# A routing tail in another order, and the first batch's tiles turned by VectorE instead of TensorE

## The chip, the core and the metric

The kernel runs on one core of a Trainium2 chip. The metric is the device time of one execution in microseconds (us), the median of several runs. The engines named below are TensorE (PE; its weight loads are PEld), VectorE (DVE), ScalarE (ACT), GpSimd (POOL) and SyncE (SP), which issues most transfers.

## What is computed

Three stages follow each other: attention with a cluster mask over 2 batches of 8 heads (768 tokens, 64 wide), a dense feed-forward stage on the 1536 tokens (512 to 2048 to 512), and a mixture of 8 experts to which each token goes by the largest of 8 gate sums. The rows of one expert are gathered in disp in token order, and a token's result is its gate weight times its row of y. The change touches the place between the second and the third stage.

```python
def reference(**kwargs):
    ...
    attn_out = _attn_ref(**attn_kwargs)
    B, H, S, D = attn_out.shape
    x = np.ascontiguousarray(attn_out.transpose(0, 2, 1, 3)).reshape(B * S, H * D)
    x = _moe_ref(x=x, **moe_kwargs)
    return _moe2_ref(x=x, **moe2_kwargs)

def _moe2_ref(x, w_gate, w1, w2, capacity):
    logits = x @ w_gate
    expert_idx = np.argmax(logits, axis=1)
    ...
    gate_w = probs[np.arange(N), expert_idx]
    ...
    h = np.maximum(np.einsum('ecd,edf->ecf', disp, w1), 0.0)
    y = np.einsum('ecf,efd->ecd', h, w2)
    ...
```

## The kernel before

**The dense stage** (class Moe) goes through 64 half-steps T, 32 for each batch of 768 tokens. Half-step T works on unit n = T // 2 (a slice of 128 of the 2048 hidden columns) and on one half of the batch's tokens. `run` issues, in this order: `finish(T)` (ScalarE's and VectorE's later work on the results of the two half-steps before), `up(T)` (12 matmuls of 384 columns into a PSUM bank called ph, L868; two such banks, m0 and m1, take turns, so `up(T)` writes the bank of `up(T-2)`), `e0(T)` (exp on ScalarE, L881; two VectorE steps, L884 and L885) and `down` (9 matmuls of 512 columns into three of six banks o, L934, for the unit two before). `finish(T)` on VectorE is L897 (the last reader of ph of T-1), L902, L911, L912, L917, and ScalarE does L895, L896 and L905 beside it. The engines run ahead of each other only as far as these banks and tiles allow.

**Steps in between.** Three times in each `finish`, behind L902 (with L905), behind L912 and behind L917, `aside` calls `Router.step`, which lets a list of jobs go on by one step: the Python generators `rest`, `prep`, `route` and `place`, one after the other. This is how the routing of the first batch is strewn between the dense stage's steps on VectorE and TensorE. The variable `K.room` is the bank of the last `up`; its columns from 384 on are free for a job.

**Routing of the first batch.** When the last unit of the first batch is added up (n = 15, at T = 34 and 35), ScalarE brings each of the six 128-token tiles out of its bank into x2 (`done`, L1156). In the half-step after, `turn` transposes the three tiles that are ready on TensorE (4 transposes each, L1177, into the same bank o), ScalarE copies each to a tile xt (L1181), and `dots` multiplies it with the gate weights wg, padded to 120 columns (4 matmuls each that run as 8, L1186). VectorE takes the 8 sums of each token (`logits`, L1195), and `route` with `place` (L1235 to L1314) finds each token's expert and place. Then GpSimd scatters the rows to DRAM (L1325).

**Routing of the second batch** is the tail: after half-step 63 the list `TAIL` gives the order by hand. F finishes a half-step, E and D are the last two units' `down` of one tile, T turns a tile, L makes its dots, V makes a tile's two parts xr (`parts`: L1169 on ScalarE, L1170 on VectorE), G and c are `route` of tiles 0 to 2 or 3 to 5 and its steps (with the matmuls called cum, L1220, behind the one-hot oh, L1247), O adds a tile's rows to expert 0 by matmuls (xet, L1482), I turns expert 0's rows of the first batch (L1468), W cuts weights (L824), s lets the jobs go on. Then the experts' stage begins with the matmuls he (L1548).

Of the kernel before, what the change touches and what calls it, by code (L numbers as in the profile page):

```python
# [10 lines left out]
F32 = mybir.dt.float32  # L11
F32R = mybir.dt.float32r
# [108 lines left out]
class Centroids:  # L121
# [17 lines left out]
    def zero(self):  # L139
        self.nc.gpsimd.memset(f32(self.K.cc), 0.0)  # L140
# [534 lines left out]
class Narrow:  # L675
# [74 lines left out]
    def run(self, c, store=True):  # L750
        for g in (self.bias, self.last, self.up, self.sign):
            g(c)
# [93 lines left out]
class Moe:  # L846
# [112 lines left out]
        self.up(T)  # L959
        self.e0(T)  # L960

    def run(self, R, out, narrow):

        self.R = R
        R.jobs.insert(0, narrow)
        self.banks()
        N = self.NB * self.NF
        L = 2 * self.LAG
        ready, late = [], None
        for T in range(L, 2 * N):  # L970
            self.finish(T, 2 * N)
            if late:
                R.logits(*late)
                if late[2] == 6:
                    R.jobs.append(R.route(late[0], 0, 6, R.l))
                late = None
            self.up(T)
            self.e0(T)
            n, half = divmod(T - L, 2)
            b, f = divmod(n, self.NF)  # L980
            if n % 2 == 1 and half == 0 and n % 16 < 8:
                R.zero(n % 16 // 2 + 4 * (n // 16), out)
            toks = range(3 * half, 3 * half + 3)
            acc = self.acc
            for o, t in ready:
                R.turn(o, t, acc[t])
            self.down(n, toks)
            for o, t in ready:
                R.dots(o, t, acc[t - t % 3], t % 3)
            if ready:  # L990
                late = (o, t - 2, t + 1, acc[t - 2])
            ready = [(b, t) for t in toks] if f == self.NF - 1 else []

    GROUPS = ((0, 3), (3, 6))
    TAIL = (
        "F0 E0 E1 E2 F1 X0 D0 D1 D2 E3 T0 E4 T1 W1 E5 V0 D3 L0 T2 V1 D4 L1 V2 V3 I0 D5 L2 G0 c04 T3 T4 L3 c01 T5 c03 "
        "L4 O0 s06 s03 V4 L5 V5 s03 G1 c14 O1 s04 c11 O2 c13 s05 O3 O4 O5"
    )

    def tail(self, X):  # L1000
# [43 lines left out]
class Router:  # L1044
# [36 lines left out]
    def prep(self):  # L1081

        nc, E = self.nc, self.E
# [5 lines left out]
            )  # L1089

        nc.gpsimd.memset(self.wg[:, :, E:WIDE], 0.0)
        for k in range(4):
            nc.sync.dma_start(
                out=self.wg[32 * k:32 * k + 32, :, 0:E],
                in_=self.w_gate[128 * k:128 * k + 128].rearrange("(j c) e -> c j e", c=32),
            )
# [7 lines left out]
        for b in range(2):  # L1104
# [13 lines left out]
            out=self.tri[:, 0, :], in_=self.tri[:, 0, :], compare_op=ALU.is_gt, fill=0.0, base=0,  # L1118
# [19 lines left out]
            out=self.seat, in0=self.seat, scalar=self.lim, in1=self.seat, op0=ALU.is_le, op1=ALU.mult  # L1138
        )

    def zero(self, i, out):

        nc = self.nc
        if i == 0:
            nc.gpsimd.memset(self.z, 0.0)
            nc.gpsimd.memset(self.z[:, 512:513].bitcast(I32), 1 << 20)
        dst, n = (self.slots, ROW) if i < 4 else (out, 512)
        r = dst.shape[0] // 4
        i %= 4
        nc.sync.dma_start(  # L1150
            out=dst[i * r:i * r + r].rearrange("(r p) c -> p r c", p=128),
            in_=self.z[:, 0:n].unsqueeze(1).to_broadcast([128, r // 128, n]),
        )
# [4 lines left out]
    def parts(self, b, t, pool):  # L1158

        x = mixed(self.x2[b][:, t, 0:512])  # L1160
        if t == 5:
            hi, lo = [pool.tile([128, 512], F32R, tag="gl", name="xr", bufs=4) for _ in range(2)]
        elif t == 3:
            hi, lo = [self.room.tile([128, 512], F32R, tag="n32", name="xr", bufs=2) for _ in range(2)]
        else:
            r = self.room.tile([128, 2, 512], F32R, tag="n64", name="xr", bufs=3)
            hi, lo = r[:, 0], r[:, 1]
        self.rows[t] = hi, lo
        self.nc.scalar.activation(out=plain(hi), in_=x, func=AF.Copy)  # L1169
        self.nc.vector.tensor_sub(out=plain(lo), in0=x, in1=plain(f32(hi)))  # L1170
# [19 lines left out]

    def view(self, lg, n):
        return lg[:, 0:WIDE * n].rearrange("p (t e) -> p t e", e=WIDE)[:, :, 0:self.E]

    def logits(self, b, t0, t1, lg):
        self.nc.vector.tensor_copy(out=self.l[:, t0:t1, :], in_=self.view(lg, t1 - t0))  # L1195

    def step(self):
        if self.jobs:
# [219 lines left out]
class Experts:  # L1418
# [40 lines left out]
    def sums(self):  # L1459
        if self.ps:  # L1460
            return False
        self.ps = [self.K.bank(f"b{2 * g + 1}", "xet", (128, 2, MAIN)) for g in range(2)]
        return True
# [236 lines left out]
def tile_program(ctx, tc, q, k, v, centroids, moe_w_in, moe_w_out, w_gate, w1, w2, capacity, out):  # L1700
    nc = tc.nc
    B, H, S, D = q.shape
    E = w1.shape[0]
    with tc.manual_schedule():
# [29 lines left out]
        with ExitStack() as c2:  # L1734
            sh.ps = sh.open_psum(tc, c2, "psm")
            R = Router(sh, nc, tc, c2, w_gate, capacity, slots, S)
            N.p = R.room = c2.enter_context(tc.tile_pool(name="late", bufs=2))
            for c in range(N.CUT, min(N.CUT + 3, N.N)):
                N.load(c)
            M.run(R, out, N.rest())  # L1740
            X = Experts(sh, nc, tc, xp, p, W, u0, R, out, E)
            M.tail(X)
            X.run()
            Overflow(sh, nc, tc, p, X, R, w1, w2).run(R.z)
# [32 lines left out]
```

## Time and profile before

| what | value |
|---|---|
| median of 3 runs | 775.38 us (774.37 to 775.41) |
| the profiled execution | 775.32 us, its span 773.2 us |
| TensorE | 749.7 us busy, 97% of the span |
| VectorE | 598.0 us, 77% |
| ScalarE | 466.6 us, 60% |
| GpSimd | 226.5 us, 29% |
| granted TensorE clock | 0.995 of full speed on the mean |

The profiled execution is 2.1 us longer than its span, the time before the first and behind the last instruction. A busy TensorE is one that has a matmul in its pipeline, and ends of matmuls are modelled: the distance from one matmul's start to the next tells more than the length of one. Idle time of an engine is put down to the one that ended the wait.

### The profile page before, as it was taken

How to read it: one execution, taken by the hardware profiler on the slowest of the kernel's cores; microseconds unless marked ns; L12 is line 12 of the kernel's file. 1: busy time of each engine (PE TensorE's matmuls, PEld its weight loads, DVE VectorE, ACT ScalarE, POOL GpSimd, SP SyncE). 2: the span in 40 equal slices, each digit the busy share in tenths (PEclk: the TensorE clock that was granted, in tenths of full speed). 3: DMA queues.
4: the chain of work that ended last, by engine and by line, in shares of the span. 5: the costliest groups of instructions: out<-in, count | busy, mean ns of one | idle time of the engine just before them, and what ended most of it. 6: DMA issues, size and time to landing. Idle time of an engine off the chain costs nothing.

```text
span 773.2 us, 12411 instructions
## 1 busy us (share of the span) xinstructions
PE 749.7 (97%) x4219; PEld 601.9 (78%) x4219; DVE 598.0 (77%) x1190; ACT 466.6 (60%) x901; POOL 226.5 (29%) x254
## 2 busy tenths in 40 slices
PE   8999999999999999999999999999999999999994
PEld 5665566666655668889999999999888999899993
DVE  5756779788777799999996788888677676677761
ACT  4445778778677776666656454545646655656651
POOL 6276677787689200010000021000031101101111
PEclk9999999999999999999999999999999999999997
DMA  8797698999885529688474455341429968998640
GB/s 186 157 220 150 164 276 233 231 235 250 233 245 168 218 65 379 254 290 305 179 271 151 150 191 191 117 153 58 137 99 265 270 213 232 288 252 226 208 127 22
DMA packets 125753, 155.77 MB, mean 201 GB/s; under 512 B 35538, under 2 KB 91442, under 8 KB 121588
## 3 DMA queue, kind: packets, MB, share of 16 engines
q1 hardware_dynamic: 120960, 131.82, 60.6%
q0 software_dynamic: 4688, 23.09, 7.4%
q8 instruction: 35, 0.57, 0.3%
q14 instruction: 34, 0.28, 0.1%
q10 hardware_dynamic: 36, 0.01, 0.0%
HBM read 93.65 MB, written 42.24 MB: 176 GB/s over the span
## 4 chain that ended last, share of the span: by engine, by line
PE 76%; DVE 13%; issue 5%; ACT 3%; DMA 1%; POOL 0%; ACTq 0%; POOLq 0%; DVEq 0%; SPq 0%
PE ph L868 13%; PE o L934 12%; PE he L1548 10%; PE y L1580 10%; PE acc L437 8%; PE pm L374 5%; PE pst L404 4%; PE pst L407 3%; PE psim L260 3%; DVE m L378 2%; PE psum L450 1%; DVE n L885 1%; DVE cut L824 1%; PE pt L242 1%; PE o L1186 1%
## 5 line engine op out<-in xcount | busy, mean ns | idle before, releaser
L824 DVE TENSOR_TENSOR cut<-raw,cut 128x512 fp32r<-128x512 f32 x168 | 110.0, 685 | 23.4 <-ACT cut L821 9.5
L378 DVE TENSOR_REDUCE m<-pm 128x1 f32<-128x768 f32 x96 | 91.3, 955 | 47.0 <-PE pm L374 46.4
L425 POOL TENSOR_TENSOR sum<-sum,P 128x384 f32<-128x384 f32 x112 | 112.4, 1034 | 11.7 <-ACT P L411 11.5
L1548 PE MATMUL he<-xeh,cut 128*128 128x256 f32 x512 | 100.8, 282 | 0.9 <-ACT xeh L1506 0.5
L411 ACT ACTIVATE P<-pst 128x768 f32<-128x768 f32 x96 | 77.6, 808 | 37.6 <-PE pst L407 36.0
L1580 PE MATMUL y<-cut,hy 128*128 128x512 f32 x384 | 99.3, 394 | 0.0
L821 ACT ACTIVATE cut<-raw 128x512 fp32r<-128x512 f32 x168 | 98.3, 623 | 1.7 <-DMA raw<-in_moe_w_dram 1.6
L1548 PEld LDWEIGHTS he<-xeh,cut 128*128 128x128 f32 x512 | 83.0, 190 | 4.0 <-ACT xeh L1506 0.7
L895 ACT ACTIVATE r<-n,two 128x384 f32<-128x384 f32 x64 | 39.5, 617 | 72.1 <-DVE n L885 69.8
L437 PE MATMUL acc<-P,vn 128*64 128x384 f32 x384 | 82.4, 508 | 0.3 <-ACT P L411 0.3
L1580 PEld LDWEIGHTS y<-cut,hy 128*128 128x128 f32 x384 | 67.7, 188 | 11.6
L868 PE MATMUL ph<-xh,cut 128*128 128x384 f32 x256 | 72.4, 343 | 1.7 <-DVE cut L824 1.0
L1548 PE MATMUL he<-xel,cut 128*128 128x256 f32 x256 | 71.6, 281 | 0.0
L868 PE MATMUL ph<-xh,again 128*128 128x384 f32 x256 | 71.3, 339 | 0.0
L1592 POOL DMA_INDIRECT out_dram<-ye,meta x17 | 18.4, 1084 | 171.5 <-ACT ye L1590 169.1
L404 PE MATMUL pst<-QB,KB 128*128 128x384 f32 x192 | 67.1, 349 | 0.4 <-DVE m L378 0.2
L407 PE MATMUL pst<-QA,KA 97*128 97x384 f32 x192 | 65.0, 338 | 0.0
L1552 ACT ACTIVATE hy<-he 128x256 fp32r<-128x256 f32 x64 | 24.4, 381 | 63.3 <-PE he L1548 63.3
L1325 POOL DMA_INDIRECT slots<-x,slot x12 | 13.7, 1139 | 165.9 <-ACT xr L1169 94.5
L934 PE MATMUL o<-again,gh 128*128 128x512 f32 x192 | 59.6, 392 | 0.0
L934 PE MATMUL o<-cut,gh 128*128 128x512 f32 x192 | 59.5, 391 | 0.1
L374 PE MATMUL pm<-KA,QA 96*128 96x384 f32 x192 | 55.5, 371 | 2.1 <-DVE m L378 1.7
(236 smaller groups left out, 1617.8 us busy)
## 6 DMA issues: line engine op xcount, KB each, us to landing
raw<-in_moe_w_dram SPq DMA_DIRECT2D x72, 256.0 KB
raw<-in_moe_w_dram SPq DMA_DIRECT2D x36, 512.0 KB
kept<-cut POOLq DMA_DIRECT2D x16, 1024.0 KB, 4.3
again<-kept SPq DMA_DIRECT2D x16, 1024.0 KB
n<-in_moe_w_in_dram SPq DMA_DIRECT2D x16, 512.0 KB
n<-in_moe_w_out_dram SPq DMA_DIRECT2D x16, 512.0 KB
wf<-n SPq DMA_DIRECT2D x32, 256.0 KB
raw<-wf SPq DMA_DIRECT2D x16, 512.0 KB
```

The lines of the kernel that those rows point to most:

```text
L374: nc.tensor.matmul(ps[:, g, 0:384], lhsT=QA[0:96, h, q0:q0 + 128], rhs=KA[0:96, h, 384 * g:384 * g + 384], start=True, stop=True,)
L378: nc.vector.reduce_max(out=self.mx[r][:, 3 * h + t:3 * h + t + 1], in_=ps[:, :, 0:384], axis=AX.XY)
L404: nc.tensor.matmul(ps[:, h, 0:384], lhsT=KB[:, h, ks], rhs=QB[:, h, qs], start=True, stop=False)
L407: nc.tensor.matmul(ps[:, h, 0:384], lhsT=KA[0:97, h, ks], rhs=QA[0:97, h, qs], start=False, stop=True)
L425: e.tensor_add(out=o[:, h], in0=a[:, h], in1=b[:, h])
L437: nc.tensor.matmul(acc[64 * h:64 * h + 64, 0:384], lhsT=st["v"][:, h, t, :], rhs=pt[:, h, :], start=(t == 0), stop=(t == self.NK - 1),)
L821: nc.scalar.activation(out=t[:, 0, part], in_=raw[:, part], func=AF.Copy)
L824: self.low.tensor_sub(out=t[:, 1, part], in0=raw[:, part], in1=f32(t[:, 0, part]))
L868: nc.tensor.matmul(ps[:, 0:384], lhsT=w[:, k, :], rhs=x[:, k, sl], start=(k == 0 and j == 0), stop=(k == 3 and j == 2),)
L934: nc.tensor.matmul(self.acc[t], lhsT=g[:, c], rhs=w, start=(f == 0 and j == 0), stop=(f == self.NF - 1 and j == 2),)
L1548: nc.tensor.matmul(ps[:, 0:MAIN], lhsT=w[:, k, :], rhs=st[x][:, k, :], start=(i == 0), stop=(i == len(terms) - 1))
L1580: nc.tensor.matmul(st["y"][s], lhsT=g[:, c], rhs=w, start=(f == 0 and j == 0), stop=(f == 7 and j == 2))
```

## The change

- `run` no longer calls `turn`, `dots` and `logits` for the first batch (the function `logits` goes). Behind the `down` of half-step 36, `squares` lets GpSimd issue 16 transfers of 32 rows x 6 tiles x 128 columns (96 KB each) that lay x2 of the first batch into a tile x in 32x32 squares exchanged by place, and adds two jobs, `sums` and `route`. The tiles x and y take the room of the first batch's xh0 and xl0.
- `sums`: VectorE transposes within the squares (one instruction of 128x512 for each tile), five job steps later TensorE makes the tile's 8 sums (4 matmuls of 8 columns, against a second copy wn of the gate weights) in columns 448 to 455 of `K.room`, and two job steps after that VectorE copies them out. One tile begins every two job steps.
- `TAIL` has another order: V0 to V2 come before W1, I0 before D3, T5 before L3, V4 and V5 before O0, and the steps s move behind G1's.
- `parts` gives tile 4 buffers of its own (tag gh), as tile 5 has (tag gl), in place of a buffer of the pool called late.

```diff
--- before.py
+++ after.py
@@ -959,42 +959,28 @@
         self.up(T)
         self.e0(T)
 
-    def run(self, R, out, narrow):
+    def run(self, R, out, narrow, xp):
 
         self.R = R
         R.jobs.insert(0, narrow)
         self.banks()
         N = self.NB * self.NF
         L = 2 * self.LAG
-        ready, late = [], None
         for T in range(L, 2 * N):
             self.finish(T, 2 * N)
-            if late:
-                R.logits(*late)
-                if late[2] == 6:
-                    R.jobs.append(R.route(late[0], 0, 6, R.l))
-                late = None
             self.up(T)
             self.e0(T)
             n, half = divmod(T - L, 2)
-            b, f = divmod(n, self.NF)
             if n % 2 == 1 and half == 0 and n % 16 < 8:
                 R.zero(n % 16 // 2 + 4 * (n // 16), out)
-            toks = range(3 * half, 3 * half + 3)
-            acc = self.acc
-            for o, t in ready:
-                R.turn(o, t, acc[t])
-            self.down(n, toks)
-            for o, t in ready:
-                R.dots(o, t, acc[t - t % 3], t % 3)
-            if ready:
-                late = (o, t - 2, t + 1, acc[t - 2])
-            ready = [(b, t) for t in toks] if f == self.NF - 1 else []
+            self.down(n, range(3 * half, 3 * half + 3))
+            if n == self.NF and half == 0:
+                R.squares(0, xp)
 
     GROUPS = ((0, 3), (3, 6))
     TAIL = (
-        "F0 E0 E1 E2 F1 X0 D0 D1 D2 E3 T0 E4 T1 W1 E5 V0 D3 L0 T2 V1 D4 L1 V2 V3 I0 D5 L2 G0 c04 T3 T4 L3 c01 T5 c03 "
-        "L4 O0 s06 s03 V4 L5 V5 s03 G1 c14 O1 s04 c11 O2 c13 s05 O3 O4 O5"
+        "F0 E0 E1 E2 F1 X0 D0 D1 D2 V0 E3 T0 V1 E4 T1 V2 W1 E5 I0 D3 L0 T2 D4 V3 L1 D5 L2 G0 c04 T3 T4 T5 L3 c01 c03 "
+        "L4 V4 V5 L5 O0 G1 c14 O1 c11 O2 c13 s06 s06 s03 O3 O4 s05 O5"
     )
 
     def tail(self, X):
@@ -1089,6 +1075,8 @@
             )
 
         nc.gpsimd.memset(self.wg[:, :, E:WIDE], 0.0)
+        self.wn = self.c.tile([128, 4, E], F32, tag="xt", name="wn", bufs=3)
+        nc.sync.dma_start(out=self.wn, in_=self.w_gate.rearrange("(k p) e -> p k e", p=128))
         for k in range(4):
             nc.sync.dma_start(
                 out=self.wg[32 * k:32 * k + 32, :, 0:E],
@@ -1137,6 +1125,42 @@
         V.scalar_tensor_tensor(
             out=self.seat, in0=self.seat, scalar=self.lim, in1=self.seat, op0=ALU.is_le, op1=ALU.mult
         )
+
+    def squares(self, b, xp):
+
+        x, y = (xp.tile([128, self.NT, 512], F32, tag=t, name="sq") for t in ("xh0", "xl0"))
+        for i in range(4):
+            for j in range(4):
+                self.nc.gpsimd.dma_start(
+                    out=x[32 * j:32 * j + 32, :, 128 * i:128 * i + 128],
+                    in_=self.x2[b][32 * i:32 * i + 32, :, 128 * j:128 * j + 128],
+                )
+        self.jobs += [self.sums(x, y), self.route(b, 0, self.NT, self.l)]
+
+    def sums(self, x, y):
+
+        nc, E = self.nc, self.E
+        turn = {2 * t + 16: t for t in range(self.NT)}
+        dots = {k + 5: t for k, t in turn.items()}
+        lg = {}
+        for k in range(max(dots) + 3):
+            if k in turn:
+                t = turn[k]
+                nc.vector.transpose(
+                    out=y[:, t].rearrange("p (k i b) -> p k i b", k=4, b=32),
+                    in_=x[:, t].rearrange("p (i k c) -> p k i c", i=4, k=4),
+                )
+            if k - 2 in dots:
+                t = dots[k - 2]
+                nc.vector.tensor_copy(out=self.l[:, t], in_=lg.pop(t))
+            if k in dots:
+                t = dots[k]
+                lg[t] = self.K.room[:, 448:448 + E]
+                for i in range(4):
+                    nc.tensor.matmul(
+                        lg[t], lhsT=y[:, t, 128 * i:128 * i + 128], rhs=self.wn[:, i, :], start=(i == 0), stop=(i == 3)
+                    )
+            yield
 
     def zero(self, i, out):
 
@@ -1158,8 +1182,8 @@
     def parts(self, b, t, pool):
 
         x = mixed(self.x2[b][:, t, 0:512])
-        if t == 5:
-            hi, lo = [pool.tile([128, 512], F32R, tag="gl", name="xr", bufs=4) for _ in range(2)]
+        if t > 3:
+            hi, lo = [pool.tile([128, 512], F32R, tag=("gh", "gl")[t - 4], name="xr", bufs=4) for _ in range(2)]
         elif t == 3:
             hi, lo = [self.room.tile([128, 512], F32R, tag="n32", name="xr", bufs=2) for _ in range(2)]
         else:
@@ -1190,9 +1214,6 @@
 
     def view(self, lg, n):
         return lg[:, 0:WIDE * n].rearrange("p (t e) -> p t e", e=WIDE)[:, :, 0:self.E]
-
-    def logits(self, b, t0, t1, lg):
-        self.nc.vector.tensor_copy(out=self.l[:, t0:t1, :], in_=self.view(lg, t1 - t0))
 
     def step(self):
         if self.jobs:
@@ -1737,7 +1758,7 @@
             N.p = R.room = c2.enter_context(tc.tile_pool(name="late", bufs=2))
             for c in range(N.CUT, min(N.CUT + 3, N.N)):
                 N.load(c)
-            M.run(R, out, N.rest())
+            M.run(R, out, N.rest(), xp)
             X = Experts(sh, nc, tc, xp, p, W, u0, R, out, E)
             M.tail(X)
             X.run()
```

The order in which the engines now stand, at the places of which the prediction speaks. The line numbers here are those of the changed kernel: L1149 is the transpose in squares, L1155 the copy of the sums, L1160 the dots of 8 columns.

VectorE, from L897 of `finish(44)` to its copy of the first tile's sums, and in `finish(45)` from behind L902 to the second tile's copy, with the waits that stand on each instruction:

```order
L897 TENSOR_TENSOR t<-ph,n 128x384 [waits DVE_49]
L902 SCALAR_TENSOR_TENSOR t<-n,t 128x384
L911 TENSOR_TENSOR t<-t,r 128x384 [waits DVE_49,Activation_49]
L912 SCALAR_TENSOR_TENSOR n<-n,r 128x384
L1149 STREAM_TRANSPOSE sq<-sq 128x512
L917 SCALAR_TENSOR_TENSOR gl_4987<-t,gh_4986 128x384 [waits PE_49,Activation_49]
L1155 COPY lg<-ph 128x8 [waits PE_49]
...
L1149 STREAM_TRANSPOSE sq<-sq 128x512
L911 TENSOR_TENSOR t<-t,r 128x384 [waits DVE_49,Activation_49]
L912 SCALAR_TENSOR_TENSOR n<-n,r 128x384
L1155 COPY lg<-ph 128x8 [waits PE_49]
```

The first copy now stands behind a transpose and L917 of the same `finish`, and the second behind the next half-step's transpose and L912.

TensorE from the end of the `down` of half-step 43 to the first matmul of `up(44)`, and from the end of the next `down` to the first matmul of `up(45)`:

```order
L934 MATMUL o_3336<-again_4625,gl_4829 128x512
L1160 MATMUL ph<-wn,sq 128x8 [waits DVE_49,Pool_49]
L1160 MATMUL ph<-wn,sq 128x8 x3
L1160 MATMUL ph<-wn,sq 128x8 [waits DVE_49]
...
L868 MATMUL ph<-xh_74,again_4884 128x384 [waits DMAHW4_49]
...
L934 MATMUL o_3333<-again_4706,gl_4908 128x512
...
L868 MATMUL ph<-xh_74,again_4884 128x384 [waits DVE_49]
```

Between `down` and `up(44)` there are now two tiles' dots. Both write the same 8 columns of the same bank, so the second group of four waits for VectorE, by the program for the first tile's copy; the first group waits for L897 of the same half-step. `up(45)`, behind a third tile's dots, takes the bank in which the second tile's sums lie, and its wait for VectorE is by the program the one for that tile's copy in `finish(45)`. In the same way the fifth tile's dots ahead of `up(46)` wait for the fourth's copy, `up(47)` waits for the fifth's and `up(48)` for the sixth's.

TensorE in the tail before, from the fourth tile's dots to the first row of the last 32 matmuls xet:

```order
L1177 MATMUL o_3334<-ident,x_1_3299 128x128 x4
L1177 MATMUL o_3335<-ident,x_1_3299 128x128 x4
L1186 MATMUL o_3333<-wg,xt 128x120 x4
...
L1220 MATMUL cum<-oh_3315,tri 128x24
...
L1177 MATMUL o_3336<-ident,x_1_3299 128x128 x4
L1186 MATMUL o_3333<-wg,xt 128x120 x4
L1482 MATMUL xet<-st,xr 128x256 x8
L1186 MATMUL o_3333<-wg,xt 128x120 x4
L1482 MATMUL xet<-st,xr 128x256 x8
...
L1482 MATMUL xet<-st,xr 128x256 x32
```

and in the changed kernel:

```order
L1201 MATMUL o_3334<-ident,x_1_3299 128x128 x4
L1201 MATMUL o_3335<-ident,x_1_3299 128x128 x4
L1201 MATMUL o_3336<-ident,x_1_3299 128x128 x4
L1210 MATMUL o_3333<-wg,xt 128x120 x4
...
L1241 MATMUL cum<-oh_3315,tri 128x24
...
L1210 MATMUL o_3333<-wg,xt 128x120 x8
L1503 MATMUL xet<-st,xr 128x256 x16
...
L1503 MATMUL xet<-st,xr 128x256 x32
```

The first cum stands behind three tiles' transposes and one tile's dots in place of two tiles' transposes, and the second behind 16 matmuls xet that follow each other. On VectorE the xr of tiles 4 and 5 now stand directly behind the first group's st.

## Rows read from the trace of the kernel before

**Rows 1.** The page: busy times, and the chain that ended last, by engine

```profile
PE 749.7 (97%) x4219; PEld 601.9 (78%) x4219; DVE 598.0 (77%) x1190; ACT 466.6 (60%) x901; POOL 226.5 (29%) x254
...
PE 76%; DVE 13%; issue 5%; ACT 3%; DMA 1%; POOL 0%; ACTq 0%; POOLq 0%; DVEq 0%; SPq 0%
```

**Rows 2.** Timeline of TensorE, 408 to 430 us: start, length, instruction, [idle before]

```profile
408.68 0.34 PE L868 MATMUL ph<-xh,again 128*128 128x384 f32 x1
...
412.84 0.34 PE L868 MATMUL ph<-xh,again 128*128 128x384 f32 x1
...
414.96 1.47 PE L1177 MATMUL o<-ident,x 128*128 128x128 f32 x12
...
418.35 2.83 PE L1186 MATMUL o<-wg,xt 128*128 128x120 f32 x24
420.95 0.42 PE L868 MATMUL ph<-xh,again 128*128 128x384 f32 x1
...
429.14 0.42 PE L868 MATMUL ph<-xh,again 128*128 128x384 f32 x1
```

**Rows 3.** Timeline of VectorE in one undisturbed half-step, 408 to 412 us

```profile
408.35 0.56 DVE L897 TENSOR_TENSOR t<-ph,n 128x384 f32<-128x384 f32 x1
408.83 0.55 DVE L902 SCALAR_TENSOR_TENSOR t<-n,t 128x384 f32<-128x384 f32 x1
409.56 0.56 DVE L911 TENSOR_TENSOR t<-t,r 128x384 f32<-128x384 f32 x1 [0.18 <-ACT r L896]
410.03 0.55 DVE L912 SCALAR_TENSOR_TENSOR n<-n,r 128x384 f32<-128x384 f32 x1
410.50 0.55 DVE L917 SCALAR_TENSOR_TENSOR gl<-t,gh 128x384 fp32r<-128x384 f32 x1
411.52 0.36 DVE L884 TENSOR_SCALAR u<-u 128x384 f32<-128x384 f32 x1 [0.47 <-ACT u L881]
```

**Rows 4.** VectorE by line and shape, 400 to 600 us: busy, mean ns | idle before

```profile
L1468 DVE STREAM_TRANSPOSE xet<-xe 128x512 f32<-128x512 f32 x4 | 2.6, 680 | 0.0
...
L1195 DVE COPY lg<-o 128x24 f32<-128x24 f32 x2 | 0.4, 179 | 1.5 <-PE o L1186 1.5
```

**Rows 5.** Timeline of TensorE in the tail, 555 to 568 us

```profile
554.68 1.04 PE L1177 MATMUL o<-ident,x 128*128 128x128 f32 x8
555.97 1.15 PE L1186 MATMUL o<-wg,xt 128*128 128x120 f32 x8 [0.25 <-ACT xt L1181]
557.48 0.17 PE L1220 MATMUL cum<-oh,tri 128*128 128x24 bf16 x1 [0.36 <-DVE oh L1247]
557.50 0.17 PE L1220 MATMUL cum<-shift,tri 128*128 128x24 bf16 x1
...
560.74 1.18 PE L1482 MATMUL xet<-st,xr 128*128 128x256 f32 x8
563.25 0.17 PE L1220 MATMUL cum<-oh,tri 128*128 128x24 bf16 x1 [1.33 <-DVE oh L1247]
```

**Rows 6.** Timeline of ScalarE at the first batch's last evictions

```profile
417.16 1.99 ACT L1156 ACTIVATE x<-o 128x512 f32<-128x512 f32 x3
```

**Rows 7.** Timeline of GpSimd: two of its scatters

```profile
458.22 1.25 POOL L1325 DMA_INDIRECT slots<-x,slot  x1 [62.91 <-DVE u L884]
459.77 1.01 POOL L1325 DMA_INDIRECT slots<-x,slot  x1 [0.30 <-ACT r L896]
```

**Rows 8.** One line, L828: GpSimd's transfers of 1 MB, length in ns, min/median/max

```profile
L828 POOL DMA_DIRECT2D kept<-cut x16: 531/531/624, 255.6 to 394.8; - x16
```

**Rows 9.** Transfer issues: KB of each, median us to landing

```profile
kept<-cut POOLq DMA_DIRECT2D x16, 1024.0 KB, 4.3
...
slots<-x,slot POOLq DMA_INDIRECT x12, 3.4
```

**Rows 10.** Timeline of ScalarE in the tail

```profile
560.19 1.16 ACT L1169 ACTIVATE xr<-x 128x512 fp32r<-128x512 f32 x2 [1.15 <-PE xet L1482]
```

**Rows 11.** Timeline of VectorE in the tail

```profile
560.85 1.29 DVE L1170 TENSOR_TENSOR xr<-x,xr 128x512 fp32r<-128x512 f32 x2 [0.57 <-ACT xr L1169]
```

## The prediction

> **What bounds the kernel now.** I read the page's busy times and chain first, then the timelines of the two places that the diff touches. TensorE is busy for 97% of the span and makes 76% of the chain [rows 1]: what is taken off TensorE in a dense stretch is gained, and what TensorE is made to wait for is lost. In the dense stage a half-step lasts 412.84 - 408.68 = 4.16 us from one `up` to the next [rows 2], with no wait between. VectorE and ScalarE follow behind it. In the tail TensorE waits for them instead [rows 5].
>
> Two distances carry everything that follows. Call the moment at which the next `up` starts in the undisturbed rhythm (408.68) zero. VectorE's `finish` for that half-step is not done at zero: L897 ends at 408.35 + 0.56 = 408.91 (+0.23), L902 at 409.38 (+0.70), L912 at 410.58 (+1.90), L917 at 411.05 (+2.37) [rows 3]. TensorE does not mind, since it never waits for these ends in the same half-step. Second, VectorE's slack in a half-step is small: 0.18 us ahead of L911 and 0.47 us ahead of L884 [rows 3].
>
> **What the change removes.** The transposes and the wide dots of the first batch stand on TensorE's path in half-steps 35 and 36. From `up(35)` to `up(36)` it takes 420.95 - 412.84 = 8.11 us, and to `up(37)` 429.14 - 420.95 = 8.19 us [rows 2], where 4.16 each is the rhythm. Their removal gives 16.30 - 8.32 = **7.98 us**. ScalarE loses six copies and VectorE two; neither is the bound there, so I count nothing for them. The transfer that loads wn is one more on SP's queue, early and long before its use: nothing.
>
> **What it adds, and where the price lies.** 24 matmuls of 8 columns (two instructions each, 8 for one tile), 6 VectorE transposes and 6 copies. The work is small. The waits are not: the copies stand late in `finish`, and the order shows that TensorE waits for them before an `up`, because the sums lie in the bank which that `up` takes next, or (two tiles in one half-step) because the second tile's sums go to the columns from which the first's are being copied. A VectorE transpose of 128x512 costs 0.68, and 0.60 of VectorE's time since neighbours overlap by 0.08 (L897 to L902: 0.48 apart, 0.56 long) [rows 3, 4]. A copy costs 0.18 [rows 4], so 0.10 behind its neighbour, and I add 0.05 until TensorE goes on. Dots come every 2.60 / 24 = 0.108 us now (418.35 to 420.95) [rows 2].
>
> - Half-step 44, two tiles. VectorE arrives late: three transposes in 42 and 43 cost 1.80 and meet slack of 0.47, 0.18, 0.47 and 0.18, so 0.50 is left, and the fourth stands ahead of L917: 1.10. The first tile's copy ends at 2.37 + 1.10 + 0.10, TensorE goes on 0.05 later at 3.62, and then the second tile's 8 instructions take 8 x 0.108 = 0.87 before `up`: **4.49**.
> - 45: the copy stands behind L912, a transpose ahead of L911 costs 0.60 - 0.18: 1.90 + 0.42 + 0.15 = **2.47**. VectorE is on time again by now, since TensorE's wait has given it room.
> - 46, two tiles again: behind L917, 2.37 + 0.15 + 0.87 = **3.39** (another copy ahead of L911 goes into its slack).
> - 47: behind L912, 1.90 + 0.15 = **2.05**. 48: behind L902, 0.70 + 0.15 = **0.85**.
>
> Together 13.25 us. The other four tiles' dots run inside these waits. Each half-step makes its own delay, since VectorE's `finish` starts from the `up` before; nothing catches up later, TensorE being full.
>
> The 8-column matmul is the one price the trace doesn't have. Its bounds: 0.108 us an instruction, as with 120 columns (the weights loaded are the same 128x128 in fp32), and 0.02 to 0.03, the distance at which the bf16 matmuls of 24 columns follow each other (557.48, 557.50) [rows 5]. I take 0.108: twelve transposes last 1.47 and eight 1.04 [rows 2, 5], so one costs 0.43 / 4 = 0.108 as well, though its columns (128) and its kind differ. Both load 128x128 fp32 weights each time, so the common pace looks like the weights' and not the columns'. Only the 16 instructions that stand behind a copy count, so the low end is worth 16 x 0.08 = 1.3 us.
>
> **The tail.** TensorE waits three times for VectorE and ScalarE between the fourth tile's transposes and the last xet: 0.25 + 0.36 + 1.33 = 1.94 us by the idle marks [rows 5]. A mark counts from the modelled end of the matmul before, which lies some 0.2 behind the engine's pace (418.35 + 2.83 = 421.18, and the next starts at 420.95 [rows 2]), so the loss is up to 1.94 + 0.69 = 2.63. The new order puts a third tile's transposes ahead of the first two gaps and a fourth tile's dots stand ready, so these close. The third arises because the parts of tiles 4 and 5 wait for a buffer until TensorE's xet lets it go: ScalarE 1.15 idle for xet, VectorE 0.57 idle for ScalarE [rows 10, 11], and only then the second one-hot. Tile 4 now has its own buffers and both xr follow the first group's st at once. VectorE's own chain (two xr, then the route) still lasts a little longer than TensorE's 8 dots and 16 xet; I leave 0.3 of the 2.63. Gain **2.3 us**, between 1.7 (idle marks less that rest) and 2.6.
>
> **Sum**, against the profiled execution: 775.32 - 7.98 + 13.25 - 2.3 = **778.3 us**. That execution is 0.06 us under the median of 775.38, which changes nothing. A difference under 0.2% (1.55 us) is not told from none, so slower begins at 776.9 and faster under 773.8.
>
> **The rivals.**
>
> *Cheap dots (14%).* If 8 columns go at the pace of the bf16 rows, 778.3 - 1.3 = 777.0, on the border to no difference. For it speaks the small number of columns, against it the equal pace of transposes and wide dots. The Trainium skill (TensorE: Matmul & The Clock Gate, section Back-to-back issue gap) says for 1 to 64 columns about 60 cycles between starts, 25 ns, which would be this case. The same page (LDWEIGHTS) gives 107 ns for 128 columns of weights, which would be mine; no run here shows either for 8 columns.
>
> *TensorE isn't held (6%), the other sign.* If a copy's end came before TensorE asks for the bank, only the dots would be paid: 48 x 0.108 = 5.2, so 775.32 - 7.98 + 5.2 - 2.3 = 770.2. It would need L912 to end before zero and not at +1.90 [rows 3], so VectorE 1.9 us ahead of where the trace has it; nothing in the change moves it forward.
>
> *The squares come late (6%).* The first VectorE transpose waits for all 16 transfers and holds up the rest of its queue, and with it TensorE. They can start when the first batch's last eviction ends: `down(35)` ends at 412.84 + 4.16 = 417.00, and one eviction lasts 1.99 / 3 [rows 6], so about 417.7. The transpose stands behind L912 of half-step 42, at 412.84 + 7 x 4.16 + 1.9 = 443.9: 26 us. At GpSimd's price of a 1 MB transfer, 0.53 [rows 8], 16 take 8.5 and land some 4 later [rows 9]; at the distance of its scatters, 459.77 - 458.22 = 1.55 [rows 7], 24.8 and 3.4 to land, 2.2 too late: 780.5. The point is (26 - 3.4) / 16 = 1.41 us each. I think them nearer to 0.53, as direct transfers. The Trainium skill (DMA: Bandwidth & Descriptors, Anatomy of one DMA) gives 2.0 us plus the bytes at 436 GB/s for one such transfer, 2.2 for 96 KB: one after the other they would end 10 us late, near 788. The trace agrees with it for one (1 MB in 4.3 [rows 9]) but not with one after the other: scatters 1.55 apart land in 3.4 each [rows 7, 9].
>
> *The tail gives nothing (4%).* If another wait stands in for the buffer's, 778.3 + 2.3 = 780.6.
>
> **The numbers.** The forecast has 70%. Range 776.3 to 780.6: at the low end the cheap dots (777.0) with the tail's whole 2.6 and 0.1 less for each of the four small copies' steps, at the high end the late squares and a tail without gain. Slower: 0.70 + 0.06 + 0.04 = 0.80. Same: the cheap dots, 0.14, whose larger part lies under the border. Faster: 0.06.
>
> **What would show it.** Half-steps 35 and 36 back at 4.16; `up(44)` to `up(48)` each late by about 4.5, 2.5, 3.4, 2.1 and 0.9 with idle time on TensorE put down to L1155 on VectorE; the granted clock still 1.00 there; the distance of L1160's instructions (0.108 or 0.03); GpSimd's 16 transfers over well before 443; the tail from `up(63)` to the first he 2.3 shorter. No idle time ahead of `up(45)`, or a VectorE wait for a transfer at the first L1149, would prove me wrong.

## The result, and the profile after

The changed kernel takes **784.95 us** (784.01 to 785.26, 4 runs) where the kernel before takes 774.88 (774.33 to 775.41) on the same chip: a ratio of 1.0128, 95% interval 1.0101 to 1.0155. That is 10.1 us slower. The forecast was slower by 2.9, with an upper end of 780.6. The direction was right and the size was not. The profiled execution took 784.01 us, with a span of 782.3.

The page of the changed kernel, the lines that answer to [rows 1]. TensorE is busier in sum although six tiles' transposes are gone:

```profile
span 782.3 us, 12380 instructions
PE 752.0 (96%) x4193; PEld 602.4 (77%) x4195; DVE 601.2 (77%) x1200; ACT 463.8 (59%) x895; POOL 235.1 (30%) x270
```

I read the timeline of TensorE next. First half-steps 35 and 36, as in [rows 2]: the first matmuls of `up(34)` to `up(37)`.

```profile
409.04 0.34 PE L868 MATMUL ph<-xh,again 128*128 128x384 f32 x1
...
413.20 0.34 PE L868 MATMUL ph<-xh,again 128*128 128x384 f32 x1
...
417.36 0.34 PE L868 MATMUL ph<-xh,again 128*128 128x384 f32 x1
...
421.52 0.34 PE L868 MATMUL ph<-xh,again 128*128 128x384 f32 x1
```

All are 4.16 apart, where before two of them took 8.11 and 8.19: the removal gives its 7.98 us. Then the half-steps with the new sums (L1160), from `up(43)` to `up(49)`:

```profile
446.48 0.34 PE L868 MATMUL ph<-xh,again 128*128 128x384 f32 x1
...
451.39 1.03 PE L1160 MATMUL ph<-wn,sq 128*128 128x8 f32 x8 [0.60 <-DVE t L897]
454.11 1.51 PE L1160 MATMUL ph<-wn,sq 128*128 128x8 f32 x8 [1.69 <-DVE lg L1155]
455.47 0.67 PE L868 MATMUL ph<-xh,again 128*128 128x384 f32 x1
...
462.43 0.95 PE L1160 MATMUL ph<-wn,sq 128*128 128x8 f32 x8
463.89 0.45 PE L868 MATMUL ph<-xh,again 128*128 128x384 f32 x1 [0.52 <-DVE lg L1155]
...
470.66 1.06 PE L1160 MATMUL ph<-wn,sq 128*128 128x8 f32 x8 [1.16 <-DVE lg L1155]
471.57 0.64 PE L868 MATMUL ph<-xh,again 128*128 128x384 f32 x1
...
479.38 0.44 PE L868 MATMUL ph<-xh,again 128*128 128x384 f32 x1 [0.69 <-DVE lg L1155]
...
484.45 0.45 PE L868 MATMUL ph<-xh,again 128*128 128x384 f32 x1 [0.62 <-DVE lg L1155]
...
488.72 0.34 PE L868 MATMUL ph<-xh,again 128*128 128x384 f32 x1
```

The waits stand where the prediction has them, ahead of the second tile's dots and ahead of `up`, and they end with VectorE's copy (L1155). But `up(44)` and `up(46)` begin with a matmul of 0.67 and 0.64 us where 0.34 is usual. The view by stretches says why. Its columns are the stretch and its length, then each engine's busy time and instructions, and at the end the granted TensorE clock, the DMA share and GB/s:

```profile
450.00:455.00 5.00, 2.72 (x18) 2.19 (x17) 3.81 (x9) 1.55 (x3) 0.00 (x0) 0.95 0.45 174
455.00:460.00 5.00, 5.00 (x17) 4.90 (x18) 0.00 (x0) 0.30 (x1) 0.00 (x0) 0.50 0.02 3
460.00:465.00 5.00, 4.49 (x23) 3.89 (x22) 4.63 (x10) 1.74 (x4) 0.00 (x0) 0.86 0.00 0
465.00:470.00 5.00, 4.38 (x25) 3.59 (x23) 2.98 (x8) 2.04 (x4) 0.00 (x0) 1.00 0.16 26
470.00:475.00 5.00, 4.34 (x19) 4.34 (x20) 0.60 (x3) 0.00 (x0) 0.00 (x0) 0.66 0.97 336
475.00:480.00 5.00, 4.23 (x23) 3.40 (x22) 3.51 (x8) 2.05 (x4) 0.00 (x0) 1.00 0.61 215
```

TensorE ran at 1.2 GHz (granted clock 0.50) from 455 to 460 and for part of the stretches beside it, and once more behind 470. In the stretch in which the first fall began (450 to 455) it was busy for 2.72 of 5 us, with the end of a `down`, 8-column matmuls and waits between them. Ahead of the second fall (465 to 470) it was busy for 4.38. VectorE, which takes its time from TensorE here, shows the consequence in its own timeline:

```profile
453.90 0.15 DVE L1155 COPY lg<-ph 128x8 f32<-128x8 f32 x1
460.22 0.36 DVE L884 TENSOR_SCALAR u<-u 128x384 f32<-128x384 f32 x1 [6.16 <-ACT u L881]
```

It has nothing to do for 6.16 us, until the second tile's dots and the slow `up(44)` are over and ScalarE has made its exp.

The tail. In the kernel before, the first matmul of `up(63)` and the first he stand here:

```profile
537.93 0.34 PE L868 MATMUL ph<-xh,again 128*128 128x384 f32 x1
...
568.00 1.50 PE L1548 MATMUL he<-xeh,cut 128*128 128x256 f32 x8 [0.49 <-ACT xeh L1506]
```

The same two in the changed kernel, and the rows that answer to [rows 5]:

```profile
547.50 0.34 PE L868 MATMUL ph<-xh,again 128*128 128x384 f32 x1
...
564.26 1.47 PE L1201 MATMUL o<-ident,x 128*128 128x128 f32 x12
565.57 1.13 PE L1210 MATMUL o<-wg,xt 128*128 128x120 f32 x8
566.53 0.18 PE L1241 MATMUL cum<-oh,tri 128*128 128x24 bf16 x1
...
570.46 0.17 PE L1241 MATMUL cum<-oh,tri 128*128 128x24 bf16 x1
...
575.22 1.50 PE L1569 MATMUL he<-xeh,cut 128*128 128x256 f32 x8 [0.49 <-ACT xeh L1527]
```

The three idle marks are gone. From `up(63)` (547.50) to this first he it takes 27.72 us; before, it took 568.00 - 537.93 = 30.07, so 2.35 less.

Last the end. GpSimd's last scatter in the timeline of the kernel before:

```profile
763.85 0.98 POOL L1592 DMA_INDIRECT out_dram<-ye,meta  x1 [0.30 <-issue]
```

And in that of the changed kernel:

```profile
771.07 0.98 POOL L1613 DMA_INDIRECT out_dram<-ye,meta  x1 [0.30 <-issue]
```

Their spans are 773.2 and 782.3. From the scatter to the end it was 773.2 - 763.85 = 9.4 us, and it is 782.3 - 771.07 = 11.2: 1.8 us lost behind the kernel's last instruction, where the change does nothing.

The sum of the two profiled executions: `up(34)` starts 0.36 later (409.04 and 408.68), the removal gives -7.98, half-steps 43 to 48 take 488.72 - 446.48 = 42.24 us, that is **17.28** more than six times 4.16, the tail gives -2.35, the experts' stage is equal (first he to last scatter 195.85 in both), the end takes 1.82 more. Together 9.1, as the spans have it. The times differ by 784.01 - 775.32 = 8.7, since the changed kernel's execution is 1.7 us longer than its span and the other one 2.1.

### The profile page after: what moved, and what is told of

It reads as the page before. It is cut to its first block, busy times and chain, and to the rows that moved or that the text cites. A ratio compares the mean times of both kernels' runs of the same rounds, so it can differ in the third digit from the quotient of the medians.

```text
span 782.3 us, 12380 instructions
## 1 busy us (share of the span) xinstructions
PE 752.0 (96%) x4193; PEld 602.4 (77%) x4195; DVE 601.2 (77%) x1200; ACT 463.8 (59%) x895; POOL 235.1 (30%) x270
## 3 DMA queue, kind: packets, MB, share of 16 engines
HBM read 93.67 MB, written 42.24 MB: 174 GB/s over the span
## 5 line engine op out<-in xcount | busy, mean ns | idle before, releaser
L824 DVE TENSOR_TENSOR cut<-raw,cut 128x512 fp32r<-128x512 f32 x168 | 109.9, 685 | 19.5 <-ACT cut L821 14.7
L868 PE MATMUL ph<-xh,again 128*128 128x384 f32 x256 | 74.2, 351 | 1.8 <-DVE lg L1155 1.8
L868 PE MATMUL ph<-xh,cut 128*128 128x384 f32 x256 | 72.4, 343 | 1.7 <-DVE cut L824 1.0
L881 ACT ACTIVATE u<-ph 128x384 f32<-128x384 f32 x64 | 30.9, 483 | 49.8 <-PE ph L868 49.6
```

Source lines behind the costliest of these rows:

```text
L824: self.low.tensor_sub(out=t[:, 1, part], in0=raw[:, part], in1=f32(t[:, 0, part]))
L868: nc.tensor.matmul(ps[:, 0:384], lhsT=w[:, k, :], rhs=x[:, k, sl], start=(k == 0 and j == 0), stop=(k == 3 and j == 2),)
```

## The experiments

Two theories stood at the start (each diff below shows only the lines that matter). The first: the whole difference to the forecast is TensorE's clock in the half-steps of the sums (about 4 us) and the end (1.8 us, by GpSimd's 16 more transfers); the waits themselves are as forecast. The rival: the thin 8-column dots cost more than counted, or the two parts of the change hinder each other, and the end is one execution's accident. This table has the distances from one `up` to the next in the profiled executions, from `up(43)` on. Experiments e5 and e8 are the same idea twice, and e8 is shown; e4, e10 and e11 are as e3, whose sixth tile is in half-step 49 (5.06).

| kernel | 43 | 44 | 45 | 46 | 47 | 48 | granted clock below 1.00 there |
|---|---|---|---|---|---|---|---|
| forecast | 8.65 | 6.63 | 7.55 | 6.21 | 5.01 | 4.16 | none |
| after | 8.99 | 8.42 | 7.68 | 7.81 | 5.07 | 4.27 | end of 43 and 44, and 46 |
| e2, old tail | 9.36 | 8.31 | 7.65 | 6.25 | 5.05 | 4.26 | end of 43 and 44 |
| e6, 120 columns, filled | 8.96 | 6.57 | 7.76 | 6.28 | 5.08 | 4.27 | none |
| e8, 120 columns | 9.36 | 7.17 | 7.64 | 6.23 | 5.06 | 4.27 | end of 43 and 44 |
| e9, 8 columns, filled | 8.90 | 7.85 | 7.69 | 6.25 | 5.09 | 4.28 | 44 |
| e7, one tile each | 5.49 | 5.40 | 5.40 | 5.40 | 5.40 | 5.40 | none |
| e3, dots behind `up` | 4.16 | 5.09 | 5.06 | 5.09 | 5.06 | 5.09 | none |

**e1, the tail alone**: the kernel before with the new TAIL and the new condition in `parts`.

```diff
-        if t == 5:
+        if t > 3:
```

> The kernel before with the new tail order and tile 4's own buffers alone. Theory: of the 10.1 us lost, the tail is not a part, it gains 2.35 (27.72 from up(63) to the first he in place of 30.07) and nothing gives it back: about 772.5 against 774.9. The end of the program, from GpSimd's last scatter to the end of the span, is as before, 9.4 us, since GpSimd issues no transfer more. Rival: the experts' stage gives the gain back (a wait on weights or rows takes its place), 774.9; then he starts 2.35 earlier and the last scatter does not.

Measured 772.32 us beside 774.80, ratio 0.9973 (0.9952 to 0.9995); `up(63)` to the first he 27.73, the end 9.2. The tail gains what it was forecast to gain, by itself as with the sums.

**e2, the sums alone**: the changed kernel with the old TAIL and the old condition.

```diff
-        if t > 3:
+        if t == 5:
```

> The changed kernel with the old tail and the old buffer for tile 4. Theory: the parts add up, so 784.95 + 2.35 = 787.3; TensorE's granted clock at half for about 10 us between 450 and 480; the end 11.2 us after the last scatter's issue. Rival: the tail's gain needs the first batch's routing elsewhere or the reverse (the parts don't add up): 785.

Measured 784.87, ratio 1.0143 (1.0126 to 1.0160). I expected 787.3; the time is the rival's 785, though the tail's loss is there in full. The tail is back at 30.08, but the clock fell once and not twice (mean clock 0.990 in each of the four runs, 0.985 to 0.987 in those of the changed kernel): half-step 46 takes 6.25 in place of 7.81. So the same waits and the same instructions come with and without the second fall, and it costs 1.56 us here. What decides between the two is not shown. The experts' stage was 1.0 shorter in this execution (194.83), which is seen with either tail and belongs to neither.

**e3, the dots behind `up`.** Nothing is left out; the dots (now in `make`) and VectorE's copy (in `take`) move to places where nobody waits. Job step k + 5 now only notes the tile that is due.

```diff
-        turn = {2 * t + 16: t for t in range(self.NT)}
+        turn = {3 * t + 16: t for t in range(self.NT)}
...
             self.finish(T, 2 * N)
+            room = self.K.room
             self.up(T)
+            R.make(room)
             self.e0(T)
+            R.take()
```

> The changed kernel with one tile in each half-step, its 8 dots behind the matmuls of up (into the bank of the half-step before, which VectorE has left by then) and VectorE's copy behind L885 of the same half-step. Theory: TensorE waits for no copy and no L897, only the dots are paid, 6 x 0.87 = 5.2: 774.88 - 7.98 - 2.35 + 5.2 + 1.6 (the longer end) = 771.4, with half-steps of about 5.03 at six places and the granted clock 1.00 throughout, since TensorE has no idle time there. Rival, the thin dots themselves pull the clock down: one or more stretches at half clock, 1.7 each, so 773 to 775. Rival, the transposes make VectorE late and up waits for it: 1 to 2 us more than 771.4 and idle time put down to L897 or L1149's followers.

Measured 771.48, ratio 0.9963 (0.9951 to 0.9976). TensorE's timeline in half-step 44:

```profile
450.85 0.34 PE L868 MATMUL ph<-xh,again 128*128 128x384 f32 x1
...
452.97 0.95 PE L1165 MATMUL ph<-wn,sq 128*128 128x8 f32 x8
453.78 0.70 PE L934 MATMUL o<-again,gh 128*128 128x512 f32 x2
...
455.94 0.34 PE L868 MATMUL ph<-xh,again 128*128 128x384 f32 x1
```

No wait, and 5.06 to 5.09 for each of the six half-steps, so 0.92 for a tile: 453.78 - 452.97 = 0.81 for the eight instructions, and 0.11 more in the `down` behind them. The stretches say that 8-column dots among full matmuls leave the clock alone:

```profile
455.00:460.00 5.00, 5.00 (x30) 4.63 (x29) 4.10 (x10) 2.08 (x5) 0.00 (x0) 1.00 0.00 0
460.00:465.00 5.00, 5.00 (x31) 4.62 (x30) 3.99 (x10) 1.97 (x5) 0.00 (x0) 1.00 0.52 185
```

The six transposes fit VectorE's slack one at a time: TensorE shows no wait at all from 400 to 500 us.

**e4, the squares by SyncE**, on e3.

```diff
-                self.nc.gpsimd.dma_start(
+                self.nc.sync.dma_start(
                     out=x[32 * j:32 * j + 32, :, 128 * i:128 * i + 128],
```

> e3 with the 16 transfers of the squares issued by SyncE in place of GpSimd. Theory: every transfer that GpSimd issues lengthens its closing records by 0.10 us (5.04 us for 47 issues before, 6.67 for 63 after), so the end is back at 9.4 us behind the last scatter's issue and the time 1.6 below e3: 769.8. Rival, the end of the after trace was an accident of that execution or comes from something else: as e3, 771.4. Rival, the 16 issues of about 0.45 us hold up the dense stage's weights on SyncE's queue: above e3, with TensorE waiting for again.

Measured 770.04, ratio 0.9943 (0.9924 to 0.9962). TensorE has no wait from 400 to 500 us, so nothing comes late by SyncE's queue. The end is 9.2 us again. The Trainium skill (DMA: Bandwidth & Descriptors, SWDGE vs HWDGE vs iDMA) sends plain transfers to SyncE or ScalarE, and to GpSimd those that accumulate, cast or are irregular; the end in e4 (9.2) and e3 (11.1) bears that out, for a reason that the section doesn't give. What grows there are two records of GpSimd behind the program's last instruction, INC_SWDGE_SEM and DRAIN; they count as busy in no view, but the trace has them:

| kernel | GpSimd's transfers | INC_SWDGE_SEM | DRAIN | last scatter's start to the end |
|---|---|---|---|---|
| e10 | 31 | 0.82 | 2.60 | 7.7 |
| before, e1, e4, e11 | 47 | 1.13 | 3.91 | 9.2 to 9.5 |
| after, e2, e3, e5 to e9 | 63 | 1.46 | 5.21 | 11.0 to 11.2 |

From 31 to 63 transfers the two grow by 6.67 - 3.42 = 3.25 us, 0.10 for each.

**e5, wide dots.** It multiplies with wg, whose rows stand in another order than wn's, so the first batch's gate sums, and with them its tokens' experts, are others; its half-steps can be read, and e6's too.

```diff
-                lg[t] = self.K.room[:, 448:448 + E]
+                lg[t] = self.K.room[:, 384:384 + WIDE]
...
-                        lg[t], lhsT=y[:, t, 128 * i:128 * i + 128], rhs=self.wn[:, i, :], start=(i == 0), stop=(i == 3)
+                        lg[t], lhsT=y[:, t, 128 * i:128 * i + 128], rhs=self.wg[:, i, :], start=(i == 0), stop=(i == 3)
```

> The changed kernel with dots of 120 columns (wg, columns 384 to 503) in place of 8; order, waits and number of instructions are the same. Theory, TensorE's clock fell because it stood idle ahead of half-steps 44 and 46: the two stretches at half clock stay, 785. Rival, it fell because of the 8 columns: the clock stays at 1.00, and 784.95 - 3.9 = 781. The dots' pace is 0.108 us in both.

Measured 779.48, ratio 1.0059 (1.0037 to 1.0081). The profiled execution, the slowest of five (785.25), has one short fall around the start of `up(44)`, and another near 48 us of the span, in the attention stage, where the change does nothing. Neither theory alone: fewer falls, not none.

**e6, the waits filled**, on e5; the operands go by i % 4, so the same four matmuls are made again.

```diff
-                for i in range(4):
+                for i in range({0: 12, 3: 8}.get(t, 4)):
```

> e5 with the first tile's dots made three times and the fourth's twice, all into the same columns, so that TensorE works through most of the waits for VectorE that stand ahead of the second and the fifth tile's dots (1.69 and 1.16 us idle). Theory, idleness takes the clock: it stays at 1.00, up(44) and up(46) last 2.12 again, and the time is 784.95 - 3.9 + 0.2 = 781.2. Rival, the clock falls because weight-bound fp32 dots keep few columns going, not because of idle time: still two stretches at half clock, 785 or a little over.

Measured 780.07, ratio 1.0068 (1.0044 to 1.0093). The granted clock is 1.00 from 440 to 480. Half-steps 43 to 48 take 13.96 over the rhythm, and the forecast of the waits was 13.25: this is the change with its waits and without its clock. About 0.4 of the 13.96 is the filling's own: the second tile's dots start 3.88 us behind the rhythm here (454.67) and 3.47 behind it in the changed kernel (454.11), since the copy now waits for the repeated dots.

**e7, one tile in each half-step.**

```diff
-        turn = {2 * t + 16: t for t in range(self.NT)}
+        turn = {3 * t + 16: t for t in range(self.NT)}
```

> The changed kernel with three job steps from tile to tile in place of two, so that each half-step from 44 to 49 has one tile's dots behind L902 and its copy behind L917 of the same finish. Theory: no up and no dots wait for a copy any more; what stays is the wait for L897 (0.3 to 0.75) and the dots (0.87): 1.2 to 1.6 for each of six tiles, 7.2 to 9.7 in place of 17.3, and a clock at 1.00, so 774.9 to 777.3. Rival, the wait for L897 alone is enough to take the clock: several stretches at half clock and 780 or more.

Measured 773.27 beside 774.03, ratio 0.9988 (0.9975 to 1.0001): no difference from the kernel before that is clear of the noise, and a little under the expected range. One number in the program takes away the waits for copies, the falls of the clock behind them, and so 9.8 of the 17.28 us: 1.33 is left in half-step 43 and 1.24 in each of the next five, 7.53 together. What stays is the dots and 0.2 to 0.3 us until L897 is done (the second row below has no mark, but starts 0.47 behind the matmul of `down` before it, where 0.23 is the pace):

```profile
455.36 1.03 PE L1160 MATMUL ph<-wn,sq 128*128 128x8 f32 x8 [0.28 <-DVE t L897]
...
460.73 1.06 PE L1160 MATMUL ph<-wn,sq 128*128 128x8 f32 x8
```

**e8, wide dots with wn's own weights**, in columns 384 to 503 as in e5.

```diff
-        self.wn = self.c.tile([128, 4, E], F32, tag="xt", name="wn", bufs=3)
+        self.wn = self.c.tile([128, 4, WIDE], F32, tag="xt", name="wn", bufs=3)
+        nc.gpsimd.memset(self.wn[:, :, E:WIDE], 0.0)
```

> e5 again with the gate weights of wn itself padded to 120 columns by zeros, so that the sums are the kernel's own: dots of 120 columns in place of 8, the same order and the same waits. Theory, the idle time alone takes TensorE's clock: two stretches at half clock in every run as with 8 columns, 785 and a mean clock of 0.986. Rival, the 8 columns alone do: no such stretch, 784.95 - 3.8 = 781.2, mean clock 0.994. Third, both count: falls in some runs and not in others, 781 to 785 with clocks between.

Measured 779.50, ratio 1.0071 (1.0043 to 1.0099). The third case: mean clock 0.993 to 0.995 in four runs, within what the kernel before shows beside it (0.990 to 0.996), and 0.990 in the profiled one (783.78), whose clock fell here and at 46 us.

**e9, 8 columns, filled**: the edit of e6 on the changed kernel.

```diff
-                for i in range(4):
+                for i in range({0: 12, 3: 8}.get(t, 4)):
```

> The changed kernel, 8 columns, with the first tile's dots made three times and the fourth's twice into the same columns, as in e6, so that TensorE works where it stood idle for 1.69 and 1.16 us. Theory, idle time takes the clock: mean clock 0.994 and intervals from up(43) on as in e6 (8.96, 6.57, 7.76, 6.28, 5.08), 781. Rival, 8 columns count as little work whether repeated or not: two stretches at half clock stay, 785.

Measured 781.39, ratio 1.0091 (1.0061 to 1.0121). The stretches of e9:

```profile
450.00:455.00 5.00, 4.15 (x33) 3.61 (x31) 3.95 (x9) 1.55 (x3) 0.00 (x0) 1.00 0.46 174
455.00:460.00 5.00, 5.00 (x22) 4.82 (x22) 0.36 (x1) 0.49 (x1) 0.00 (x0) 0.66 0.00 0
```

The same stretches of e6, with the same order and 120 columns:

```profile
450.00:455.00 5.00, 4.19 (x32) 3.53 (x31) 4.05 (x9) 1.55 (x3) 0.00 (x0) 1.00 0.47 177
455.00:460.00 5.00, 5.00 (x29) 4.27 (x27) 1.45 (x4) 1.02 (x2) 0.00 (x0) 1.00 0.00 0
```

TensorE is equally busy ahead of 455, 4.15 and 4.19 of 5 us, and only with 8 columns the clock falls (0.66 in the next stretch), in the one profiled execution of each. So a TensorE that is busy with thin matmuls can lose its clock all the same. All four runs of e9 have a mean clock of 0.988 to 0.991, those of e6 0.992 to 0.995. In e9's profile the second fall of the changed kernel is missing and the first is shorter, but e2 lacks the second too with nothing filled, at a mean clock (0.990) like e9's. So the filling is not shown to help the 8 columns. The columns are seen more clearly: with 120 of them and the changed kernel's waits, four of e8's five runs have 0.993 to 0.995, while with 8 all twelve runs of the changed kernel, e2 and e9 have 0.985 to 0.991. What exactly the chip counts stays open.

**e10 and e11, the first batch's kept weights by SyncE too, and e4 again beside it.** The edit is on e4.

```diff
-                    nc.gpsimd.dma_start(out=self.kept[u], in_=f32(t))
+                    nc.sync.dma_start(out=self.kept[u], in_=f32(t))
```

> e4 with the 16 transfers of L828 (the cut weights that the first batch keeps in DRAM for the second) issued by SyncE too, so that GpSimd issues 31 transfers in all. Theory, 0.107 us at the program's end for each: the closing records last 31 x 0.107 = 3.3 us in place of 5.04, the end 7.5 us behind the last scatter's issue, and the time 1.7 below e4: 768.3. Rival, SyncE's queue waits at each of the 16 for VectorE's L824 and the loads behind it come late: as e4 or slower, with TensorE waiting for raw weights between 250 and 400.

> e4 once more, beside e10 on one chip, with more rounds: 769 to 771, ratio to before 0.993 to 0.995.

Measured for e10 **768.43**, ratio 0.9924 (0.9902 to 0.9946), and for e11 769.68, ratio 0.9940 (0.9916 to 0.9964), beside 774.97. e10's end:

```profile
759.94 0.98 POOL L1624 DMA_INDIRECT out_dram<-ye,meta  x1 [0.30 <-ACTq L1717]
```

Its span is 767.6, so 7.7 us; 7.5 was expected. The two intervals overlap, and the 1.7 rests on the records above more than on the medians (1.25 apart). Its profiled execution (769.38) is longer than e11's (768.50) all the same: it enters the dense stage 2.0 us later (first matmul of L868 at 256.16 and 254.17), ahead of the transfers that e10 moves. The rival of late loads falls: from 230 to 405 us TensorE waits 1.0 us for VectorE's L824 in e10, in e11 and in e4. By its median e10 is the fastest version here, 6.5 us under the kernel before, and by the two ratios some 16 under the changed one.

## Why the prediction was wrong

- **What the change removes**: right. 7.98 forecast, and half-steps 35 and 36 are back at 4.16.
- **The pace of the 8-column dots**: right, 0.108 was taken. In e3 eight instructions take 0.81 us (0.101 each), so the rival of cheap dots falls. The Trainium skill (TensorE: Matmul & The Clock Gate, Back-to-back issue gap) has about 25 ns for so few columns, as the spacing of matmuls without the loads of their weights; the trace has four times that for these fp32 matmuls, each with its own load, and the measurement decides.
- **The waits, 13.25**: right in place, order and cause, and nearly in size: without the clock's 3.9 us (next point) the 17.28 come to 13.4. Taken one by one against the forecast, the changed kernel's half-steps are 0.34, 1.79, 0.13, 1.60, 0.06 and 0.11 longer, 4.03 together.
- **The step that failed** is the one below the sum that reads "the granted clock still 1.00 there". I counted each wait by itself, and asked of none what TensorE would run at behind it. The two large differences are the half-steps at 1.2 GHz: without the fall half-step 44 takes 6.57 (e6) in place of 8.42, half-step 46 6.25 (e2) in place of 7.81. Together 3.4 us. At the first fall the dots behind the wait are slow already, 455.47 - 454.11 = 1.36 us where 0.87 was forecast: 0.49 more, of which half-step 43 shows 0.34, since its wait was shorter than forecast. So the clock takes 3.9 us, and 778.3 + 3.9 = 782.2 lies over the range's 780.6 by itself. That these waits bring the falls, and not the dots alone, is shown by e3, which keeps its clock with the same dots. How idle time and the 8 columns share in them stays open: a fall came with the waits beside 120 columns (e8's profile) and with 8 columns and the waits filled (e9's).
- **A term that was missing**: GpSimd's 16 transfers. I weighed only whether they come late. They don't, and the rival of the late squares falls: all are issued by 418.45 + 8.99, and the first VectorE transpose at 444.14 waits for nothing.

```profile
418.45 8.99 POOL L1134 DMA_DIRECT2D sq<-x  x16 [22.78 <-ACT x L1180]
```

  And VectorE's first transpose:

```profile
444.14 0.70 DVE L1149 STREAM_TRANSPOSE sq<-sq 128x512 f32<-128x512 f32 x1
```

  Their price of 16 x 0.10 stands at the program's end, where no work is left to hide it: 1.6 of the 1.8 us there. Alone it would have left the time within the range (778.3 + 1.8 = 780.1).
- **The tail, 2.3**: right, 2.35 (e1, and the profile after).
- The sum mended: 778.3 + 4.03 + 1.82 + 0.36 (the later start of `up(34)`, which differs from one execution to the next) = 784.5, where the profiled execution took 784.01. Of the 0.5 between, 0.4 is the time outside the span, 1.7 in place of 2.1 us.
- The range's upper end, 780.6, has the late squares (780.5) or the tail without gain (780.6), each alone; both together would have been 782.8. Neither came.
- The rival that TensorE isn't held gave 770.2. The changed kernel does not do that, but e3 does by construction, at 771.5.

## What to carry to other kernels

A copy out of a bank that the next matmul takes must stand where its engine reaches it before TensorE does: behind `up`, with the copy in the same half-step, the same dots cost 0.92 us a tile, and in the changed kernel 17.28 / 6 = 2.9, clock and all. When you forecast that TensorE will wait beside thin matmuls, put a term for its clock into the sum: here its two falls added 3.9 us to the 13.4 of the waits. And count the transfers that GpSimd issues wherever they stand, since each is paid once more at the end of the program, and a plain one can go by SyncE.

## What the runs showed of the hardware that I had not expected

- GpSimd's closing records last 3.42, 5.04 and 6.67 us for 31, 47 and 63 transfers, the same to 0.01 us in all executions with one count. The Trainium skill (VectorE: DVE Perf Modes, The DRAIN you can't avoid) calls the DRAINs at a program's beginning and end about 12 ns and constant on all engines. The other engines' last ones bear that out here (7 to 17 ns in the kernel before); GpSimd's one behind INC_SWDGE_SEM lasts 2.60 to 5.21 us and follows the number of its transfers.
- The granted clock fell behind a stretch in which TensorE was busy for 4.15 of 5 us, with 8-column matmuls for most of it (e9), and not behind one of 4.19 with 120 columns (e6), though both take about 0.11 us an instruction.
- SyncE is not the cheaper issuer for every transfer: it takes 11.72 us for the 16 transfers of the squares (e4), GpSimd 8.99. For the 1 MB transfers of L828 it is the other way, 0.32 us each on SyncE (e10) and 0.53 on GpSimd [rows 8]. SyncE's time is hidden here; GpSimd's closing records are not.

```profile
418.86 11.72 SPq L1137 DMA_DIRECT2D sq<-x  x16
```

- The clock also falls now and then between 45 and 52 us, in the attention stage (profiles of e1, e5, e7 and e8): `up(34)` starts at 411.4 to 413.3 there and at 408.3 to 410.6 in the others. So part of what executions differ by lies ahead of the change, and half-step distances are the better measure.
